# Replanning an attention kernel's VectorE tiles, normalization and TensorE load

## The chip, the cores and the metric

The kernel runs on one core of a Trainium2 chip. The metric is the device time of one execution in microseconds (us). Every timed execution comes with its span (first to last instruction) and the mean clock that TensorE was granted. The time is about 1.7 us longer than the span.

An execution is called slow when it is over 1.5% above the fastest of the same kernel. Only fast executions are compared; three executions of experiments 5 and 6 were slow and are left out.

## The reference

```python
eps = 1e-6                       # B, H, S, Dh = 1, 32, 2048, 20, bf16
qn = q / (jnp.sqrt((q * q).sum(axis=-1, keepdims=True)) + eps)
kn = k / (jnp.sqrt((k * k).sum(axis=-1, keepdims=True)) + eps)
logits = jnp.einsum('bhqd,bhkd->bhqk', qn, kn) * t[None, :, None, None]
return jnp.einsum('bhqk,bhkd->bhqd', softmax(logits, axis=-1), v)
```

There are 32 heads of 2048 x 2048 scores and almost no arithmetic per score but the exponential.

## The kernel before

The exponentials are shared between two engines. ScalarE takes them in *waves* of 3 x 512 columns, straight from TensorE's scores in `psA`. VectorE takes 3 or 4 of the 16 rows of tiles of a head: it evicts four blocks of 512 scores from `psD` (one 128x512 tile that TensorE writes) as integers, then forms the exponential by bit operations (`ee`, `ss`, `mm`, `tt`). TensorE multiplies all of them with the values into `psO` (another such tile), which VectorE transposes and divides at the end of each head. VectorE also normalizes queries and keys of later heads.

The program is not written in order. Tasks with dependencies, durations and priorities go through a list scheduler, which fixes each engine's order before the kernel is built. The change touches only priorities and one knob:

```python
class Program:
    LIGHT = 9.0
    TICK = 3.41
    LOAD = 3072.0            # TensorE columns asked of each tick
    PASSES = 10
    ...
    def schedule(self):
        heavy = set()
        choice = [t for t in self.tasks if t.rows == 0]   # single score matmuls
        for _ in range(self.PASSES):
            for t in choice:
                t.rows = 128 if t in heavy else 64
            self.list_schedule()
            pe = [t for t in self.order["PE"] if t.end > self.LIGHT]
            ...
            # walk a window of TICK us over the plan; where its work is under LOAD,
            # make single matmuls in it 128 rows wide (+256 columns each)
```

The program keeps the operands of a score in 32 of a tile's 128 rows, a row group: a 64-row matmul holds the operands of two row groups, one of them multiplied by zeros. Matmuls of 64 rows overlap: in the trace of the kernel before 565 of 1984 start 3 or 4 ns after another, and one lasts 0.39 us. A 128-row one computes the same scores from all four groups, three of them multiplied by zeros; it is there only to ask more columns of TensorE, against the half clock that the profile below shows in some stretches. That this helps was the idea of the program; experiments 2, 5 and 6 test it.

```python
    LEAD = 2.4               # heads by which normalization is due ahead
    SPREAD = 0.6             # heads over which its 12 or so steps are spread
    ...
    def add_prep(hs):
        due = hs[0] - LEAD
        def dv(name, fn, dur, deps):
            step[0] += 1
            return add("DVE", name + str(hs[0]), fn, dur, deps,
                       due + (SPREAD * (step[0] - 1) / 12 if hs[0] > 2 else 0.0))
    ...
    def add_dgroup(jg):      # one VectorE tile of head h
        due = h + (j - d0[h] + 0.3) / DVE_TILES[h] - 0.25
```

## Time and profile before

| | before |
|---|---|
| time, median of 3 (range) | 739.66 us (738.92 to 740.25) |
| the profiled execution: time, span, granted clock | 744.0 us, 742.3 us, 0.983 |
| ScalarE busy / VectorE busy | 730.0 / 724.2 us |

These are lines of the page. "tenths" are busy shares of 40 slices; PEclk is TensorE's granted clock in tenths.

```profile
span 742.3 us, 12574 instructions
PE 638.9 (86%) x4974; PEld 163.2 (22%) x4996; DVE 724.2 (98%) x1334; ACT 730.0 (98%) x546; POOL 3.2 (0%) x20
...
PEclk8799999999999999999999999999999999999999
...
ACT 94%; PE 3%; DVE 1%; POOL 0%; SPq 0%; DMA 0%; issue 0%; ACTq 0%; POOLq 0%
```

The last line is the chain that ended last: ScalarE is 94% of it. Two engines are 98% busy. The timeline of ScalarE from its first wave on (start, duration, engine, line, operation; in brackets the idle time before it and what ended it):

```profile
10.40 5.68 ACT L585 ACTIVATE p_ring<-psA 128x1536 bf16<-128x1536 f32 x4 [0.69 <-PE psA L506]
16.43 4.48 ACT L585 ACTIVATE p_ring<-psA 128x1536 bf16<-128x1536 f32 x3 [0.35 <-PE psA L506]
21.40 1.45 ACT L585 ACTIVATE p_ring<-psA 128x1536 bf16<-128x1536 f32 x1 [0.49 <-PE psA L506]
23.77 2.96 ACT L585 ACTIVATE p_ring<-psA 128x1536 bf16<-128x1536 f32 x2 [0.92 <-PE psA L506]
27.25 108.92 ACT L585 ACTIVATE p_ring<-psA 128x1536 bf16<-128x1536 f32 x81 [0.52 <-PE psA L506]
136.67 538.78 ACT L585 ACTIVATE p_ring<-psA 128x1536 bf16<-128x1536 f32 x401 [0.49 <-PE psA L506]
676.56 43.09 ACT L585 ACTIVATE p_ring<-psA 128x1536 bf16<-128x1536 f32 x32 [1.11 <-PE psA L506]
720.08 18.06 ACT L585 ACTIVATE p_ring<-psA 128x1536 bf16<-128x1536 f32 x14 [0.43 <-PE psA L506]
```

That is all: 538 waves at 1.344 us, and seven gaps after the first wave that sum to 4.3 us. In four windows of time (columns: length, then busy us and instructions of PE, PEld, DVE, ACT, POOL, then the granted clock, DMA share, GB/s) the clock is half:

```profile
14.10:27.70 13.60, 13.60 (x66) 2.42 (x66) 10.54 (x27) 11.13 (x9) 0.00 (x0) 0.50 0.40 60
133.60:137.00 3.40, 3.07 (x14) 0.76 (x15) 2.55 (x5) 2.91 (x3) 0.00 (x0) 0.50 0.71 42
672.90:676.30 3.40, 3.40 (x20) 0.64 (x20) 2.58 (x6) 2.55 (x2) 0.00 (x0) 0.50 0.02 5
717.20:720.70 3.50, 3.17 (x13) 0.61 (x13) 2.08 (x4) 3.07 (x3) 0.00 (x0) 0.51 0.00 0
```

All seven gaps lie in these stretches or end them. Note PE's busy column: in the first window TensorE is busy 13.60 of 13.60 us and does only 66 matmuls. Busy time is highest here exactly where TensorE is slowest: a score matmul lasts 0.61 to 0.63 us in the four stretches (medians), and 0.39 us between 40 and 130 us.

In the trace's clock records the stretches are 3.413 us long or, the first, four times that (13.653 us), and the granted share in them is 0.50.

VectorE has a margin. Its last tile operation and the last accumulator transpose, from the timeline of VectorE:

```profile
734.65 1.23 DVE L632 TENSOR_TENSOR tt<-xt,mm 128x2048 f16<-128x2048 f16 x1
738.64 0.72 DVE L533 STREAM_TRANSPOSE oT<-psO 128x512 f32<-128x512 f32 x1 [2.76 <-PE psO L521]
```

The last tile ends at 734.65 + 1.23 = 735.88 us; ScalarE's last wave ends at 720.08 + 18.06 = 738.14. VectorE ends 2.3 us before ScalarE. I call this difference the **VectorE margin**.

### The profile page before, as it was taken

What the parts mean: (1) busy time and instruction counts of PE and PEld (TensorE: products, weight loads), DVE (VectorE), ACT (ScalarE), POOL (GpSimd) and SP (SyncE); (2) the same over time, 40 slices, a digit from 0 to 9 for tenths busy, and PEclk for the clock granted to TensorE, in tenths of its full rate; (3) what the DMA queues carried; (4) which work ended last, traced back from release to release, by engine and by line L of the source; (5) the groups of instructions that cost most, each with busy time, mean ns of one, the idle gap of its engine ahead of it and who ended that gap; (6) DMA issues with size and microseconds to landing.
All of it is one profiled execution on the core that took longest, in us unless ns stands there. A gap on an engine that the chain in (4) does not pass through costs nothing.

```text
span 742.3 us, 12574 instructions
## 1 busy us (share of the span) xinstructions
PE 638.9 (86%) x4974; PEld 163.2 (22%) x4996; DVE 724.2 (98%) x1334; ACT 730.0 (98%) x546; POOL 3.2 (0%) x20
## 2 busy tenths in 40 slices
PE   8987888888898888898888888888889888888896
PEld 2122222222222222222222222222222222222221
DVE  8899999999999999999999999999999999999986
ACT  7899999999999999999999999999999999999997
POOL 1000000000000000000000000000000000000000
PEclk8799999999999999999999999999999999999999
DMA  5333233232233233223233323323323323330100
GB/s 62 77 41 57 50 64 46 29 61 52 52 50 48 44 61 57 55 39 52 42 61 61 50 34 54 61 46 56 55 45 46 58 44 56 58 56 19 34 1 10
DMA packets 196650, 36.10 MB, mean 49 GB/s; under 512 B 172528, under 2 KB 196592, under 8 KB 196592
## 3 DMA queue, kind: packets, MB, share of 16 engines
q1 hardware_dynamic: 196448, 35.22, 29.9%
q8 instruction: 39, 0.64, 0.4%
q14 instruction: 19, 0.16, 0.1%
q10 hardware_dynamic: 144, 0.08, 0.0%
HBM read 7.87 MB, written 2.62 MB: 14 GB/s over the span
## 4 chain that ended last, share of the span: by engine, by line
ACT 94%; PE 3%; DVE 1%; POOL 0%; SPq 0%; DMA 0%; issue 0%; ACTq 0%; POOLq 0%
ACT p_ring L585 94%; PE psA L506 1%; PE psO L521 1%; PE psD L506 1%; SPq L290 0%; DMA qk_sb<-in_q_dram 0%; DVE sq L389 0%; DVE qz L480 0%; POOL vaug L293 0%; POOL qkn L293 0%; DVE rs_sum L391 0%; DVE oT L533 0%; DVE xt L618 0%; ACTq L255 0%; DVE o_stage L543 0%
## 5 line engine op out<-in xcount | busy, mean ns | idle before, releaser
L585 ACT ACTIVATE p_ring<-psA 128x1536 bf16<-128x1536 f32 x538 | 723.1, 1731 | 5.3 <-PE psA L506 5.0
L506 PE MATMUL psA<-qz,kR 64*128 64x512 bf16 (+1 forms) x1200 | 291.2, 390 | 61.2 <-ACT p_ring L585 56.1
L618 DVE TENSOR_SCALAR xt<-psD 128x512 int16<-128x512 f32 x436 | 296.7, 680 | 10.6 <-PE psD L506 9.2
L521 PE MATMUL psO<-p_ring,vaug 128*32 128x512 bf16 x1612 | 156.7, 390 | 1.1 <-ACT p_ring L585 0.9
L506 PE MATMUL psA<-qz,qkT 64*128 64x512 bf16 x398 | 128.8, 386 | 20.5 <-ACT p_ring L585 18.7
L506 PE MATMUL psD<-qz,kR 64*128 64x512 bf16 x318 | 124.1, 390 | 10.8 <-DVE xt L618 8.3
L632 DVE TENSOR_TENSOR tt<-xt,mm 128x2048 f16<-128x2048 f16 x109 | 132.2, 1213 | 0.2
L506 PEld LDWEIGHTS psA<-qz,kR 64*128 64x128 bf16 x1210 | 63.0, 94 | 200.7 <-ACT p_ring L585 186.4
L626 DVE TENSOR_SCALAR ee<-xt 128x2048 int16<-128x2048 int16 x109 | 74.4, 683 | 0.2
L630 DVE TENSOR_SCALAR mm<-xt 128x2048 int16<-128x2048 int16 x109 | 74.4, 683 | 0.0
L628 DVE TENSOR_SCALAR ss<-xt 128x2048 int16<-128x2048 int16 x109 | 74.4, 682 | 0.0
L521 PEld LDWEIGHTS psO<-p_ring,vaug 128*32 128x32 bf16 x1612 | 40.1, 94 | 103.3 <-issue 99.3
L506 PEld LDWEIGHTS psD<-qz,kR 64*128 64x128 bf16 (+1 forms) x326 | 30.5, 93 | 81.2 <-DVE xt L618 57.1
L506 PEld LDWEIGHTS psA<-qz,qkT 64*128 64x128 bf16 (+1 forms) x402 | 31.7, 94 | 65.2 <-ACT p_ring L585 58.5
L506 PE MATMUL psD<-qz,qkT 64*128 64x512 bf16 (+1 forms) x110 | 42.5, 386 | 3.2 <-DVE xt L618 2.4
L521 PE MATMUL psO<-tt,vaug 128*32 128x512 f16 x436 | 43.9, 393 | 1.2 <-ACT p_ring L585 0.7
L521 PE MATMUL psO<-ss,vaug 128*32 128x512 f16 x436 | 43.8, 391 | 0.0
L521 PE MATMUL psO<-ee,vaug 128*32 128x512 f16 x436 | 43.6, 390 | 0.0
L389 DVE TENSOR_TENSOR sq<-qk_sb 128x640 f32<-128x640 bf16 x32 | 26.1, 814 | 0.2 <-DMA qk_sb<-in_q_dram 0.2
L391 DVE TENSOR_REDUCE rs_sum<-sq 128x32 f32<-128x640 f32 x32 | 25.7, 804 | 0.1
L533 DVE STREAM_TRANSPOSE oT<-psO 128x512 f32<-128x512 f32 x32 | 22.6, 706 | 2.8 <-PE psO L521 2.8
L417 DVE TENSOR_TENSOR qkn<-qk_sb,rs_r 128x640 bf16<-128x640 bf16 x31 | 25.2, 814 | 0.0
(43 smaller groups left out, 138.7 us busy)
## 6 DMA issues: line engine op xcount, KB each, us to landing
kR<-qkT SPq DMA_DIRECT2D x62, 96.0 KB, 2.1
qz<-qkT SPq DMA_DIRECT2D x124, 32.0 KB, 1.9
kR<-qkT SPq DMA_DIRECT2D x62, 64.0 KB, 2.0
qk_sb<-in_k_dram SPq DMA_DIRECT2D x32, 80.0 KB, 2.1
vaug<-in_v_dram SPq DMA_DIRECT2D x32, 80.0 KB, 3.3
qk_sb<-in_q_dram SPq DMA_DIRECT2D x124, 20.0 KB, 2.5
out_dram<-o_stage SPq DMA_DIRECT2D x31, 80.0 KB, 1.6
kR<-qkT SPq DMA_DIRECT2D x62, 32.0 KB, 1.9
```

The lines of the kernel that those rows point to most:

```text
L389: s1 = dv("sq", lambda e, tk, x=x: e.tensor_tensor(sq[:, :, :], x[:, :, :], x[:, :, :], ALU.mult), 0.735, lds[h] + last_sum + (q0[2:] if h ...
L391: sums.append(dv("sum", lambda e, tk, i=i: e.tensor_reduce(rs["sum"][:, 2 * R * i:2 * R * (i + 1)], sq[:, :, :], AXIS_X, ALU.add), 0.73, [ ...
L417: norm[h] = dv("norm", lambda e, tk, x=x, b=b, i=i: e.tensor_tensor(qkn[b][:, :, 0:D], x[:, :, :], bc(rs["r"][:, 2 * R * i:2 * R * (i + 1) ...
L506: return eng.matmul(dst, lhsT, mov, tile_position=(p0, 0))
L521: last = eng.matmul(psO[32 * g:32 * g + 32, :], vaug[h % NV][:, r_of(g), :], rhs_of(g), start=start, stop=False, skip_group_check=True, ti ...
L533: trO[h] = add("DVE", f"tr{h}", lambda e, tk: e.transpose(oT[:, :, :].rearrange("p r d -> p (r d)"), psO[:, :]), 0.63, [lambda: pv_users[h ...
L585: act[w] = add("ACT", f"exp{w}", lambda e, tk: e.activation(p_ring[:, p0 * 512:p0 * 512 + n], psA[:, slot * WAVE * 512:slot * WAVE * 512 + ...
L618: t1_prev[0] = add("DVE", f"t1.{j}.{g}", lambda e, tk, o=o: e.tensor_scalar(xt[sx][:, o:o + 512], psD[:, :], X_MUL, X_ADD, ALU.mult, ALU.a ...
L626: te = dv("e", lambda e, tk: e.tensor_scalar(ee[se][:, 0:w], x, 0x7C00, KE_BITS, ALU.bitwise_and, ALU.bitwise_or), 0.533, t1s + old("e", NE))
L628: t5 = dv("s", lambda e, tk: e.tensor_scalar(ss[se][:, 0:w], x, float(SHIFT - 4096), None, ALU.add), 0.533, t1s + old("s", NE))
L630: tm = dv("m", lambda e, tk: e.tensor_scalar(mm[sm][:, 0:w], x, 0x3FF, 0x3800, ALU.bitwise_and, ALU.bitwise_or), 0.533, t1s + old("m", NM))
L632: tT = dv("T", lambda e, tk: e.tensor_tensor(tt[se][:, 0:w], x.bitcast(FP16), mm[sm][:, 0:w].bitcast(FP16), ALU.mult), 1.067, [tm] + old(" ...
```

## The change

Its intent: let VectorE work further ahead of ScalarE, start normalization earlier and interleave it evenly, and ask more columns of TensorE so that its clock stays up. ScalarE and VectorE keep the same operations. The whole diff:

```diff
-    LOAD = 3072.0
+    LOAD = 3500.0
@@
-    LEAD = 2.4
-    SPREAD = 0.6
+    LEAD = 3.0
+    SPREAD = 1.0
@@ add_dgroup
-                due = h + (j - d0[h] + 0.3) / DVE_TILES[h] - 0.25
+                due = h + (j - d0[h] + 0.3) / DVE_TILES[h] - 0.8
```

## The prediction

> **What bounds the kernel now.** ScalarE. The page gives ACT 730.0 us of a 742.3 us span; the chain of waits is 94% the exponential. Its 538 waves take 723.1 us (groups of instructions): 1.344 us each. The first starts at 10.40 us, the last ends at 737.64, and 4.6 us of transpose, normalization and store follow. Between first and last wave ScalarE idles only about 4.3 us, in seven gaps, each put down to a score matmul (timeline): 0.35, 0.49, 0.92, 0.52 at 16 to 27 us, then 0.49 at 136.7, 1.11 at 676.6, 0.43 at 720.1. VectorE is as full (724.2 us), idle mostly at the start and after 700 us.
>
> The windows' clock column says why: all seven gaps fall in, or just end, stretches where TensorE was granted half its clock: about 14.1 to 27.7, 133.6 to 137.0, 672.9 to 676.3, 717.2 to 720.7 us. Each is 3.41 us or four times that[...]. Summing matmul columns from the trace (512 for a 128-row matmul, half for a 64-row one, 128 for each 32-column one), the windows just before these stretches held 2871, 2886, 2880 and 3072 columns, while the median full-clock window held about 4280. Some 30 windows lie below 3500. The three later dips stand at head ends: there the accumulator's transpose waits for products of VectorE tiles, and the next head's products wait behind it.
>
> **What the change does.** ScalarE and VectorE keep their operations and tiles. (a) 3500 instead of 3072 columns per tick turns more single 64-row score matmuls into 128-row ones (some 42 in the trace now; I estimate 80 to 200 after). Each costs TensorE at most a 0.22 us slot no longer shared: 10 to 35 us against the 61 + 20 us in which PE waits for ScalarE before score matmuls. (b) Tiles 0.55 head earlier, normalization 0.6 earlier: VectorE is already full, so both move together and the real order changes little. But tiles gain over spread normalization and final divisions, so a head's last tile is ready before ScalarE's last wave and the transpose comes promptly. The cost: products wait in three buffers for the one accumulator, so VectorE may wait under 1 us at head ends.
>
> **Worth.** The ceiling is 4.3 us: about 735.4 us. I expect most of the three later dips to go (about 1.6 of 2.0 us), and the 13.7 us half-clock stretch at the start, worth 2.3 us, to go or shorten with a chance of about one half. New waits give back 0.3 to 0.8 us.
>
> **Prediction:** 737.2 us, 8 in 10 within 735.2 to 740.0. Faster by over 2%: 0.01; within 2%: 0.95; slower by over 2%: 0.04.
>
> **What would show it.** Clock 1.00 from 40 to 735 us (right: none or one dip; wrong: two or more). Waves still 1.344 us, 538 of them. ScalarE's idle between waves under 2.5 us. More 128-row score matmuls, 80 or more. The window before 14 us over 3100 columns and no half clock after it. Accumulator transposes within about 1 us of the head's last wave.
>
> **What would make it wrong.** Wide matmuls delaying ScalarE's scores outside half-clock stretches (new gaps on ScalarE after 40 us); VectorE blocked by full tile buffers for several us; normalization too late for a head's first wave[...].

## More of the kernel before

How many single matmuls the plan widened is read from the weight loads, listed by form (all 4996 weight loads are in the trace, while some matmul records are missing). Before, 23 + 12 + 23 + 6 = 64 are 128 rows wide:

```profile
L506 PEld LDWEIGHTS psD<-qz,kR 128*128 128x128 bf16 x23 | 2.3, 99 | 7.2 <-DVE xt L618 5.6 <-issue 0.9 <-DVE rs_a L399 0.4
L506 PEld LDWEIGHTS psA<-qz,kR 128*128 128x128 bf16 x23 | 2.2, 98 | 6.0 <-issue 4.3 <-ACT p_ring L585 1.6
L506 PEld LDWEIGHTS psA<-qz,qkT 128*128 128x128 bf16 x12 | 1.1, 96 | 4.8 <-ACT p_ring L585 3.4 <-issue 1.3
L506 PEld LDWEIGHTS psD<-qz,qkT 128*128 128x128 bf16 x6 | 0.6, 96 | 1.7 <-DVE xt L618 1.0 <-DVE rec L536 0.7
```

## The result, and the profile after

| | before | after |
|---|---|---|
| time of the first comparison, median of 4 (range) | 739.61 us (738.92 to 740.25) | 738.85 us (738.77 to 738.87) |
| ratio of mean times, 95% interval | | 0.999, 0.9972 to 1.0007 |
| larger sample: executions, median, range | 33: 739.97, 738.33 to 744.32 | 10: 738.85, 738.77 to 738.88 |
| 128-row single score matmuls (weight loads) | 64 | 252 |
| VectorE margin in the profile | 2.3 us | 2.4 us |

A ratio is the mean time of one kernel's fast runs over that of the other's fast runs of the same rounds, so it is not quite the ratio of the quoted medians. The larger sample is, for the kernel before, its runs beside the experiments on three chips; for the changed kernel, the first four runs and the six of experiment 8, which turned out to be the same program.

By the median the change is worth about 1 us of 740; the interval of the first comparison includes 1, so four executions of each alone do not show a gain. What it changes plainly is the spread: 6 us before, 0.1 us after. 27 of the 33 executions of the kernel before were slower than every one of the changed kernel, and six were faster, by about 0.4 us.

After, the page and the timeline of ScalarE:

```profile
span 737.0 us, 12540 instructions
PE 635.1 (86%) x4947; PEld 172.0 (23%) x4996; DVE 723.7 (98%) x1334; ACT 729.3 (99%) x546; POOL 3.2 (0%) x20
...
PEclk9999999999999999999999999999999999999999
...
ACT 97%; DVE 1%; PE 1%; POOL 0%; DMA 0%; SPq 0%; issue 0%; ACTq 0%; POOLq 0%
```

```profile
10.30 722.61 ACT L585 ACTIVATE p_ring<-psA 128x1536 bf16<-128x1536 f32 x538 [0.80 <-PE psA L506]
```

One line in place of eight: all 538 waves without a gap. The same four windows of time, at full clock:

```profile
14.10:27.70 13.60, 11.58 (x91) 3.19 (x95) 13.33 (x32) 13.52 (x11) 0.00 (x0) 1.00 0.41 62
133.60:137.00 3.40, 2.77 (x30) 0.74 (x28) 3.31 (x8) 3.40 (x4) 0.00 (x0) 1.00 0.64 41
672.90:676.30 3.40, 3.25 (x32) 0.84 (x24) 3.40 (x9) 3.40 (x4) 0.00 (x0) 1.00 0.00 0
717.20:720.70 3.50, 3.32 (x40) 0.83 (x32) 2.50 (x5) 3.50 (x4) 0.00 (x0) 1.00 0.07 23
```

TensorE now does 91 matmuls in the first window instead of 66, and is busy for less of it. The widened weight loads are 105 + 37 + 74 + 36 = 252:

```profile
L506 PEld LDWEIGHTS psA<-qz,kR 128*128 128x128 bf16 x105 | 10.1, 96 | 30.1 <-ACT p_ring L585 15.9 <-issue 13.6
L506 PEld LDWEIGHTS psD<-qz,kR 128*128 128x128 bf16 x74 | 7.1, 96 | 22.0 <-DVE xt L618 13.4 <-issue 3.6 <-DVE rs_u L394 2.0
...
L506 PEld LDWEIGHTS psA<-qz,qkT 128*128 128x128 bf16 x37 | 3.6, 96 | 12.0 <-ACT p_ring L585 6.4 <-issue 5.5
L506 PEld LDWEIGHTS psD<-qz,qkT 128*128 128x128 bf16 x36 | 3.4, 96 | 9.0 <-DVE xt L618 6.0 <-issue 1.4 <-DVE rs_u L394 0.7
```

And VectorE's end:

```profile
729.28 1.23 DVE L632 TENSOR_TENSOR tt<-xt,mm 128x2048 f16<-128x2048 f16 x1
733.42 0.72 DVE L533 STREAM_TRANSPOSE oT<-psO 128x512 f32<-128x512 f32 x1 [2.91 <-PE psO L521]
```

The last tile ends at 730.51, the last wave at 10.30 + 722.61 = 732.91. The margin is what it was.

Did the order move tiles ahead of ScalarE, as the change's name says? For each head I took the end of its last `tt` against the end of ScalarE's last wave with a unit of that head. The median over the heads is 0.0 us ahead before and 0.1 us behind after. The accumulator's transpose starts 2.04 us after that wave in the median before, and 1.99 us after. The plan moved; by these two measures the execution did not. VectorE is full and all its priorities moved together, which is a likely reason but was not tested.

### The profile page after: what moved, and what is told of

The parts are those of the page before. It is cut to its first block, busy times and chain, and to the rows that moved or that the text cites. A ratio compares the mean times of both kernels' runs of the same rounds, so it can differ in the third digit from the quotient of the medians.

```text
span 737.0 us, 12540 instructions
## 1 busy us (share of the span) xinstructions
PE 635.1 (86%) x4947; PEld 172.0 (23%) x4996; DVE 723.7 (98%) x1334; ACT 729.3 (99%) x546; POOL 3.2 (0%) x20
## 4 chain that ended last, share of the span: by engine, by line
ACT 97%; DVE 1%; PE 1%; POOL 0%; DMA 0%; SPq 0%; issue 0%; ACTq 0%; POOLq 0%
ACT p_ring L585 97%; PE psA L506 0%; DMA qk_sb<-in_q_dram 0%; SPq L290 0%; DVE sq L389 0%; DVE qz L480 0%; DVE xt L618 0%; PE psD L506 0%; POOL vaug L293 0%; PE psO L521 0%; POOL qkn L293 0%; DVE rs_sum L391 0%; DVE oT L533 0%; DVE mm L630 0%; ACTq L255 0%
## 5 line engine op out<-in xcount | busy, mean ns | idle before, releaser
L521 PE MATMUL psO<-p_ring,vaug 128*32 128x512 bf16 x1612 | 151.0, 385 | 4.2 <-issue 3.0
L506 PE MATMUL psA<-qz,qkT 64*128 64x512 bf16 (+1 forms) x391 | 126.3, 384 | 18.2 <-ACT p_ring L585 16.5
L506 PE MATMUL psD<-qz,kR 64*128 64x512 bf16 (+1 forms) x314 | 120.4, 384 | 7.4 <-DVE xt L618 5.0
L506 PEld LDWEIGHTS psA<-qz,kR 64*128 64x128 bf16 (+1 forms) x1210 | 67.9, 94 | 204.0 <-ACT p_ring L585 173.7
```

The source lines that it names most:

```text
L506: return eng.matmul(dst, lhsT, mov, tile_position=(p0, 0))
L521: last = eng.matmul(psO[32 * g:32 * g + 32, :], vaug[h % NV][:, r_of(g), :], rhs_of(g), start=start, stop=False, skip_group_check=True, ti ...
```

## The experiments

Theory A: the gain is the half-clock stretches that the wider matmuls remove. Theory B: the gain is the order. "Before" ran in every round beside them; its median was 740.14, 740.02 and 739.73 us in the three calls.

### 1. Only the columns

```diff
 kernel before
-    LOAD = 3072.0
+    LOAD = 3500.0
```

> The old order with only the asked TensorE columns raised from 3072 to 3500. The plan makes 461 of 974 single score matmuls 128 rows wide (64 in the kernel before, 252 in the changed one). Theory A (the clock: the small gain is the half-clock stretches that the wider matmuls take away, the order only helps to need fewer of them): no half-clock stretch between 30 and 730 us, and 738.8 us within 0.4, unless 461 wide matmuls make ScalarE wait for scores; then gaps on ScalarE at full clock, and 740 us or more. Theory B (the order: tiles ahead of ScalarE's waves take the waits at head ends away, whatever the columns): as the kernel before, 739.6 us, the half-clock stretches gone or not.

Measured: 744.9 us (744.8 to 746.5), ratio 1.0065 (1.0042 to 1.0087). Neither theory's number. There was no half clock before 736 us and ScalarE ran without a gap. Its timeline, then VectorE's last operations:

```profile
10.26 722.89 ACT L585 ACTIVATE p_ring<-psA 128x1536 bf16<-128x1536 f32 x538 [0.80 <-PE psA L506]
```

```profile
737.49 1.23 DVE L632 TENSOR_TENSOR tt<-xt,mm 128x2048 f16<-128x2048 f16 x1
...
739.44 0.72 DVE L533 STREAM_TRANSPOSE oT<-psO 128x512 f32<-128x512 f32 x1 [0.72 <-PE psO L521]
```

ScalarE is done at 733.15 us, as in the changed kernel. VectorE's last tile ends at 738.72, 5.6 us after it: the margin is -5.6 us. Half of theory A holds (the columns take the half-clock stretches away), and a cost appears that neither theory had: VectorE becomes the later engine. The page's chain still says ACT 96%, because a chain that switches engine near its end keeps most of its length on ScalarE.

This is theory C: **time is the later of two chains**. ScalarE's chain is its waves plus what the half clock makes them wait. VectorE's chain is its tiles plus what the plan makes them wait, and a plan with more wide matmuls can push it past ScalarE's.

### 2. Only the order

```diff
 changed kernel
-    LOAD = 3500.0
+    LOAD = 3072.0
```

> The changed order with the asked columns left at 3072 (65 wide in the plan). Theory A: half-clock stretches remain as in the kernel before, in some executions at the start too; 739.6 us, spread 738.9 to 740.3 or wider. Theory B: 738.8 us within 0.3, waves of ScalarE without gaps.

Measured: 739.78 us; six executions from 738.40 (clock 0.998) to 745.10 (clock 0.982), ratio 1.0002 (0.9968 to 1.0036). This is the spread of the kernel before. In the profiled one (739.7 us) the only gap on ScalarE over 0.3 us is 1.11 us at 42.60, and 38.94 to 42.35 us is its one half-clock stretch before the end:

```profile
42.60 691.24 ACT L585 ACTIVATE p_ring<-psA 128x1536 bf16<-128x1536 f32 x515 [1.11 <-PE psA L506]
```

Theory B falls; the order alone does nothing to the time that these runs can show.

### 3. Only the tiles

```diff
 kernel before
-  ... / DVE_TILES[h] - 0.25
+  ... / DVE_TILES[h] - 0.8
```

> VectorE tiles due 0.55 head earlier, normalization as before, columns 3072. Tiles now press normalization aside. If the two had to move together: some head's normalized operands come late and ScalarE waits tens of ns to some us at its start, 741 us or more, with gaps on ScalarE at full clock. If the tile shift alone is what helps (theory B): 738.8 us. Theory A: 739.6 us.

Measured: 748.23 us (747.97 to 748.51), ratio 1.0106. The slower branch of the expectation, but mostly by another road: ScalarE's gaps after 40 us are two (1.68 us at full clock, then 0.94 us), and VectorE's last tile ends at 742.40, 5.5 us after ScalarE's last wave at 736.91. Pressed aside, normalization is late, and with it the loads of later heads, which the program makes wait for its transposes. The timeline of VectorE shows it standing still for a load:

```profile
589.98 0.82 DVE L389 TENSOR_TENSOR sq<-qk_sb 128x640 f32<-128x640 bf16 x1 [2.05 <-DMA qk_sb<-in_q_dram]
```

While VectorE waits, it evicts no scores, TensorE waits for that eviction (1.94 us idle before its matmul into `psD` at 591.47 us, put down to `xt`), and ScalarE's gap of 1.68 us (to 592.10 us) follows. So the tiles can't move without normalization; the reverse doesn't hold, as experiment 4 shows.

### 4. Only the normalization

```diff
 kernel before
-    LEAD = 2.4
-    SPREAD = 0.6
+    LEAD = 3.0
+    SPREAD = 1.0
```

> Normalization due three heads ahead and spread over one head, tiles and columns as before. Theory A: 739.6 us with the half-clock stretches of the kernel before. Theory B: also 739.6, as no tile comes earlier; if normalization presses tiles aside, gaps at head ends and up to 741 us.

Measured: 741.16 us, from 738.53 (clock 0.998) to 746.40 (clock 0.980), ratio 1.0012 (0.9979 to 1.0046). The spread of the kernel before again, as theory A had it. Its profile is of a fast one (739.07 us) and has no half clock before 734 us, so the clocks of the six executions show the spread here, not the profile. With VectorE's margin at 3.3 us in it, nothing there ends late.

### 5 and 6. No widening, in the new and in the old order

```diff
 changed kernel (5)              kernel before (6)
-    LOAD = 3500.0              -    LOAD = 3072.0
+    LOAD = 0.0                 +    LOAD = 0.0
```

> The changed order with no widening at all (0 columns asked; 77 of 974 planned would have been the share for 3072). Theory A: many half-clock stretches, ten or more, each costing ScalarE 0.4 to 1.1 us: 742 to 750 us, and time falls linearly with the half-clock share over all runs. Theory B: within 0.5 us of the changed kernel's 738.8.

(The aside on 77 matmuls in it is a slip of mine; the plan of the new order with 3072 columns widens 65.)

> The old order with no widening. Theory A: like the changed order without widening, 742 to 750 us. Theory B: 740 to 741 us, slower than the changed order without widening by the same 0.8 us as the two tuned kernels differ.

Measured, fast executions: 745.8 to 751.3 us for the new order (clock 0.979 to 0.965; two slow ones at 764 left out), 744.1 to 748.2 us for the old (0.984 to 0.970; a slow one at 759.6 left out). Both are on theory A's side, the new order a little beyond its range. The ranges of the two overlap, so which order is slower is not shown, but the 0.8 us that theory B promised the new order are not there. The profile of 5 has six half-clock stretches before its last wave (47.8 us by its windows of time, fourteen times 3.41), where ten or more were expected. Five windows of time of the profile of 5, with half clock:

```profile
14.70:28.30 13.60, 13.51 (x62) 2.17 (x60) 10.63 (x25) 11.05 (x8) 0.00 (x0) 0.50 0.35 61
...
110.20:117.00 6.80, 6.80 (x38) 1.30 (x38) 5.70 (x9) 5.81 (x5) 0.00 (x0) 0.50 0.43 68
134.10:144.40 10.30, 10.21 (x51) 1.88 (x51) 8.89 (x16) 8.83 (x7) 0.00 (x0) 0.50 0.37 66
161.40:168.30 6.90, 6.72 (x39) 1.16 (x39) 5.22 (x10) 5.34 (x5) 0.00 (x0) 0.51 0.38 65
257.00:263.80 6.80, 6.80 (x41) 1.16 (x40) 4.81 (x10) 5.28 (x4) 0.00 (x0) 0.50 0.33 31
```

ScalarE's column is 1.0 to 2.6 us short in each. What the missing widening costs: experiments 5 and 2 differ in 65 widened matmuls (and in what the plan shifts for them), and in time: 745.8 to 751.3 us (slow executions left out; clock 0.979 to 0.965) against 738.4 to 745.1 us (0.998 to 0.982).

What do the weight loads show of the time before a half-clock stretch? In the profile of the kernel before, four such stretches start at 14.096, 133.562, 672.868 and 717.241 us: 35, 158 and 13 times 3.413 us apart. I cut that profile on this grid, from about 10 us after the start to 15 us before the end, and counted columns (512 for a 128 x 128 weight load, half for 64 rows, a quarter for 32 columns, spread over 0.21 us from 0.10 us after the load's start). The four full-clock pieces just before half clock held 2875, 3063, 3000 and 2878 columns; the emptiest of the other full-clock pieces held 3103. With the columns placed 0.05 us later the two groups meet (3072 against 3071). In the profile of the changed kernel, cut in the same way, pieces of about 3009 and 3071 columns were followed by full clock. So neither a limit in columns nor that columns decide at all is shown. There was no long pause either: in the piece before 133.56 us TensorE's longest gap, matmuls and weight loads taken together, was 0.73 us.

The kernel before asks 3072 of its plan. The fullest of the four pieces held 3063, so whatever the execution shifts against the plan may decide. This is the lottery, as I read it: an estimate from these counts, not shown. Asking 3500 leaves 428 columns more in the plan. In the execution it is less: in the profile of the changed kernel the two pieces above and four more were under 3500. None was followed by half clock, but ten executions of this plan are all that shows how safe it is.

### 7. Everything widened

```diff
 changed kernel
-    LOAD = 3500.0
+    LOAD = 100000.0
```

> The changed order with every single score matmul 128 rows wide (974 of 974). No half-clock stretch. If TensorE has room (theory A, work off the path): 738.8 us within 0.4. If wide matmuls delay scores: new gaps on ScalarE at full clock, each of 0.05 to 0.5 us, in total over 2 us: 741 us or more.

Measured: 753.11 us (752.7 to 753.5), ratio 1.0172. No half clock before 739 us. ScalarE's gaps are small (its timeline shows two, 0.34 and 0.17 us) and its last wave ends at 734.86 us. VectorE's last tile ends at 747.43: the margin is -12.6 us.

```profile
617.22 117.64 ACT L585 ACTIVATE p_ring<-psA 128x1536 bf16<-128x1536 f32 x88 [0.17 <-PE psO L521]
```

```profile
746.21 1.23 DVE L632 TENSOR_TENSOR tt<-xt,mm 128x2048 f16<-128x2048 f16 x1
```

So TensorE has room for ScalarE even with all 974 wide, and I was wrong about whom wide matmuls would hurt. They work against VectorE.

### 8. A tile more on VectorE, which it was not

```diff
 changed kernel
-  DVE_TILES = [4 if h % 8 in (1, 4, 6) or h == 31 else 3 ...]
+  DVE_TILES = [4 if h % 8 in (1, 4, 6) or h >= 30 else 3 ...]
```

> The changed kernel with one more tile of head 30 on VectorE, four units less on ScalarE (536 or 537 waves instead of 538: 1.8 us less). If ScalarE's wave count is the floor and VectorE's idle time after 700 us is real room: 737.0 us within 0.4. If VectorE then ends last: 738.8 to 741 us, with the last transpose waiting for its tile.

Measured: 738.84 us (738.79 to 738.88). The edit changes nothing: 30 % 8 is 6, so head 30 had four tiles already, and the program is the same instruction for instruction. It tells nothing about VectorE's room; it is a second measurement of the changed kernel, within 0.1 us.

### 9. Relief for VectorE

Experiment 1 again, with one tile of head 30 moved from VectorE to ScalarE:

```diff
 kernel before
-    LOAD = 3072.0
+    LOAD = 3500.0
-  DVE_TILES = [4 if h % 8 in (1, 4, 6) or ...]
+  DVE_TILES = [3 if h == 30 else 4 if h % 8 in (1, 4, 6) or ...]
```

> The kernel of the first experiment (old order, 3500 columns, 744.9 us) with one tile of head 30 given back from VectorE to ScalarE: ScalarE gets 1.8 us more work, VectorE 5.4 us less. Theory C (time is the later of two chains; ScalarE's end is fixed by its waves, and wide matmuls make VectorE's last tile late): faster than 744.9 by 3 to 5 us, 740.5 to 741.5 us, although the bounding engine of the page got more work. Rival (wide matmuls cost ScalarE or the clock): 746.7 us.

Measured: 740.81 us (740.78 to 740.98), 4.1 us less than experiment 1. ScalarE got more work and the kernel became faster. ScalarE has 539 waves now, still without a gap, and VectorE is early again:

```profile
10.41 724.70 ACT L585 ACTIVATE p_ring<-psA 128x1536 bf16<-128x1536 f32 x539 [0.80 <-PE psA L506]
```

```profile
731.24 1.23 DVE L632 TENSOR_TENSOR tt<-xt,mm 128x2048 f16<-128x2048 f16 x1
...
735.62 0.72 DVE L533 STREAM_TRANSPOSE oT<-psO 128x512 f32<-128x512 f32 x1 [3.15 <-PE psO L521]
```

Margin: 735.11 - 732.47 = 2.6 us. The time is the changed kernel's 738.84 plus the 1.8 us of work that moved, within 0.2 us. The weight loads show 461 wide matmuls, as many as in experiment 1, so it is not a smaller number of them that helped. Theory C stands.

### 10, 11, 12. Which part of the order makes room for VectorE

```diff
 10: kernel before, LOAD = 3500.0      11: kernel before, LOAD = 3500.0      12: changed kernel
-    SPREAD = 0.6                     -    LEAD = 2.4                       -    SPREAD = 1.0
+    SPREAD = 1.0                     +    LEAD = 3.0                       +    SPREAD = 0.6
```

> The kernel before with 3500 columns and the wider spread of normalization alone (lead and tiles as before; 276 wide in the plan). If spreading normalization is what lets VectorE bear the wide matmuls: VectorE's last tile ends before ScalarE's last wave, no half clock, 738.8 us within 0.4, all executions within 0.3. If the tile shift is needed: like the first experiment, 742 to 745 us.

> The kernel before with 3500 columns and the longer lead of normalization alone (337 wide). If spreading is what matters: VectorE's last tile ends some 5 us after ScalarE's last wave, 742.5 to 745 us, and little spread between executions. If any earlier normalization does: 738.8 us.

> The changed kernel with the old spread of normalization (0.6 head; 258 wide in the plan, its thinnest planned window 3584 columns against 3072). If the wider spread is needed with the tile shift too: VectorE late, 741 us or more. If what counts is only that VectorE ends before ScalarE, by whatever order: 738.8 us within 0.3, VectorE's last tile some 4 us before ScalarE's last wave against 2.4 in the changed kernel, no half clock.

| | time, us (range) | last tile, us | last wave, us | margin, us | wide matmuls |
|---|---|---|---|---|---|
| 1: columns alone | 744.9 (744.8 to 746.5) | 738.72 | 733.15 | -5.6 | 461 |
| 10: columns and spread | 738.83 (738.74 to 739.01) | 731.48 | 733.15 | 1.7 | 276 |
| 11: columns and lead | 745.81 (744.7 to 746.7) | 739.95 | 734.16 | -5.8 | 337 |
| 12: columns, lead and tiles | 738.58 (738.49 to 738.63) | 728.27 | 732.63 | 4.4 | 258 |
| the change: all four | 738.85 (738.77 to 738.88) | 730.51 | 732.91 | 2.4 | 252 |

Every plan of the table with a positive margin takes 738.6 to 738.85 us, every plan with a negative one is 6 to 7 us slower. No single knob of the order is needed: the spread alone does it (10), and so do lead and tile shift together without it (12); the lead alone does not (11, a little slower than its expectation said). Number 10's last wave and last tile, then number 12's VectorE end:

```profile
10.53 722.62 ACT L585 ACTIVATE p_ring<-psA 128x1536 bf16<-128x1536 f32 x538 [0.80 <-PE psA L506]
```

```profile
730.25 1.23 DVE L632 TENSOR_TENSOR tt<-xt,mm 128x2048 f16<-128x2048 f16 x1
```

```profile
727.04 1.23 DVE L632 TENSOR_TENSOR tt<-xt,mm 128x2048 f16<-128x2048 f16 x1
733.13 0.72 DVE L533 STREAM_TRANSPOSE oT<-psO 128x512 f32<-128x512 f32 x1 [4.86 <-PE psO L521]
```

By its median, 12 beats both kernels, by 0.26 us against the changed one. The ranges don't overlap, but the two ran on different chips, so 0.04% is all but nothing.

The last column holds a rival that I left untested. With another order the plan needs fewer wide matmuls to reach the same 3500 columns, and the two late plans are the two with the most. So the order may help by itself, or by sparing wide matmuls. An estimate from the margins: from 64 to 461 wide the old order loses 7.9 us of margin, from 252 to 974 (7) the new order loses 15.0, which is 0.020 and 0.021 us for each. The 209 fewer of the changed kernel would then be worth about 4 of the 8.0 us between it and experiment 1. The number is not all: 11 is as late with 337 as 1 with 461, and 3 is 5.5 us late with 61.

Where does VectorE lose its time in the bad plans? Not in long waits. Operations that follow each other freely overlap by about 0.08 us in VectorE's timeline; after 40 us, 83 operations of experiment 1 start without that overlap at a gap of under 0.1 us, 28 in the changed kernel, and many of them are the small dependent steps of the reciprocal root that stand next to each other instead of between tile operations. Summed against an overlap of 0.075 us, and without the wait for the last transpose, VectorE loses 15.1 us in experiment 1 and 8.5 us in the changed kernel. The difference, 6.6 us, is most of the 8.0 us of margin. This is a count from traces; no run separated these losses one by one.

## Why the prediction was right or wrong

**The time.** 737.2 us was forecast, within 735.2 to 740.0 and "within 2%"; 738.85 was measured. The range held, but it holds 739.61, no change at all, as well, so that says little; the central value asked for three times the gain: 2.4 us instead of 0.8. The step that failed is "The ceiling is 4.3 us: about 735.4 us". The gaps were rightly read from the profile, but they were subtracted from the median of other executions. The profiled execution took 744.0 us; of the 33 timed beside the experiments only two were slower. Its own ceiling was 744.0 - 4.3 = 739.7, and the changed kernel, at 738.85, reached it and a little more. The little more is in the trace too: waves without gaps end 1.343 us apart, and the seven waves after a gap end 5.1 us later than that in all, since such a wave does not overlap the one before it (a wave by itself lasts 1.45 us); 744.0 - 5.1 = 738.9.

The term that was mis-sized is the half-clock stretches of a typical execution. I took 4.3 us. The median execution (739.97) stands 1.6 us above the six luckiest (about 738.4, at clock 0.998 or 0.999), and the changed kernel 0.4 above these, so 1.1 us (739.97 - 738.85) was won. "New waits give back 0.3 to 0.8 us" is right in size, though from what is open (below).

That there was a gain at all is partly luck. The columns, on which the prediction counted, take 744.9 us alone (1), outside the range; the order, of which it expected little, kept VectorE from ending last.

The runs show the lottery of the half clock directly. Over the 33 executions of the kernel before, time against the length of half clock (2 x (1 - granted clock) x span) has a correlation of 0.93 and a slope of 0.25 us per us. So a quarter of the length of half clock was paid; in the first stretch of the profile before, ScalarE was busy 11.13 of 13.60 us, against 13.52 at full clock in the changed kernel. A likely reason why it was no more, not tested, is that TensorE is not the bounding engine and waits for ScalarE anyway, 61 + 20 us in the profile before.

**What bounds.** Right: ScalarE, in 1.344 us waves, with all gaps in half-clock stretches. One number was misread: the last wave ends at 738.14, not 737.64, so the tail is 4.1 us.

**The clock.** Right, and more than expected: all stretches between the first and the last wave went, the one at the start too, for which I gave one half. The sign that I had named for it, over 3100 columns in the window before 14 us, is missing: the window from 10.3 to 13.7 us held about 3009 by weight loads. That asking for more columns does it and not the order is shown by 1, 10 and 12 (no half clock before ScalarE's last wave in their profiles) against 2, 5 and 6.

**How many wide matmuls.** "80 to 200", from 42 counted; it was 252, from 64. Counting matmul records, some of which were missing, was the mistake; the weight loads are complete. The records that are missing, 22 before and 49 after, are all of wide score matmuls. It bent the column counts as well: by the weight loads 13 windows, not some 30, lie below 3500.

**"10 to 35 us against the 61 + 20 us in which PE waits".** Right for ScalarE (7: all wide, and its last wave is only 2 us later) and wrong as the whole account. It left out VectorE, which has a margin of 2 us and whose scores all pass through one tile, `psD`: the program makes each of their matmuls wait for the eviction before it, and each eviction for its matmul. In the profile before, weight loads for `psD` waited 78.5 us in all for evictions (`xt`), and evictions 9.2 us for matmuls. Columns alone cost 5 us (1).

**The order.** "Both move together and the real order changes little" is right (0.0 and -0.1 us). "But tiles gain [...] and the transpose comes promptly" is wrong: 2.04 us before, 1.99 us after, and 31 of 32 transposes over 1 us late in both. My explanation of the later dips by late transposes lent the order a gain that it doesn't have. Its worth is that VectorE ends before ScalarE at 3500 columns; how much of that is the order itself and how much the fewer wide matmuls is not shown.

**VectorE's waits** at head ends stayed under 1 us, as predicted, but for the 2.91 us before the last transpose; idle time before its evictions fell from 10.6 to 5.9 us.

**Open.** The luckiest executions of the kernel before (738.33 to 738.47) beat the changed kernel by 0.4 us. About 0.12 us is the first wave: it starts 1.87 or 1.88 us after the copies before it in the profiles with 3072 columns that I compared (before, 2, 4) and 1.99 us after them in those with 3500 (1, 9 to 12 and the changed kernel). The rest is not settled, as no such execution of the kernel before was profiled.

## What to carry to other kernels

Compare the profiled execution's time with the timed median before turning its gaps into a forecast: here the profile was of one of the slowest executions, with 4.3 us of gaps where a typical one loses about 1.6. When two engines are both 98% busy, write down which ends last and by how much; a change that frees one can push the other past it, and the chain's shares (96% ScalarE) will not tell. Look at the spread between executions: here it was 6 us with 3072 columns asked and 0.1 us with 3500, in the changed order, so asking for more was the remedy; check whom it costs (VectorE here, and 5 us of time in the old order).
